# Attention heads with values held in the array: 64x64 quadrants and row sums on VectorE

## The chip, the cores and the metric

The kernel runs on one core of one Trainium2 chip. Its time is the device time of one execution, in microseconds (us). TensorE is PE in the profile and its weight loads PEld; VectorE is DVE, ScalarE ACT, GpSimd POOL, and SyncE (SP) issues DMAs.

## The reference

One block: layer norm, attention against a given key and value cache, a gated feed-forward branch, and their product added to the input. All tensors are bfloat16.

```python
B, Sq, D = 1, 2048, 640
H, Sk, Dh = 32, 2048, 192          # F = 1536
xn = layernorm(x)
q = (xn @ wq) -> (H, Sq, Dh)
scores = einsum("hqd,hkd->hqk", q, k_cache) * Dh ** -0.5
p = softmax(scores)
o = einsum("hqk,hkd->hqd", p, v_cache)
s = o -> (Sq, H * Dh) @ wo
g = silu((silu(xn @ w1) * (xn @ w3)) @ w2)
out = x + s * g
```

## The kernel before

The work runs head by head. Of a head, the 2048 queries are cut into four query blocks (`qb`) of 512, and the 2048 keys into eight steps (`p`) of 256. Even and odd keys form two halves, `t` = 0 and 1, so a step has 128 keys in each half.

**A step.** `advance` emits it. `scores` (L484) computes keys by queries, `st2`: 128 keys on the partitions, two halves of 512 queries in two PSUM banks. The 192 channels are cut into three parts of 64; each part is one pair of matmuls, the two on the two row halves of the array (`ROWS`, partitions 0 to 63 and 64 to 127), one for each key half `t`. `weights` (L490) lets ScalarE take the exponential of the 128x1024 scores into the bf16 tile `pT2`. `values` (L530) multiplies the probabilities with the values: the probabilities are the stationary operand, 64 keys by 128 queries, and 193 columns stream through them, the 192 channels of `vt` and a column of ones (`set_ones`) that yields the row sums. It takes 16 matmuls a step, in pairs on the two row halves, and accumulates over all steps of a block into two tiles of two PSUM banks, `ob0` and `ob1`.

**Order.** TensorE, VectorE and ScalarE keep the program's order for what is wrapped in `pin`; other instructions, most GpSimd copies and DMA issues of later heads among them, are placed by the framework. The values of a step are cut into parts kept in the list `parts`; they are emitted some steps behind the scores, so that the exponential has time. PSUM has two `st2` tiles, which scores and projections share in turn.

**End of a block.** `evict` copies the one row half's sums out of PSUM on VectorE (L500), adds the other's (L501), takes the reciprocal of the row sums (L506) and writes the product into the staging tile `ostage` (L507), twice for a block. A store to DRAM (`o_scr`) follows for each pair of heads and block (L511).

**Beside it, in each block.** At step 1 `project_chunk` (L361) projects 512 queries of the next head with 20 matmuls into an `st2` tile; two casts bring them to SBUF (`qA` L363, `qF` L364, VectorE), and three GpSimd copies (L367 twice, L371) make `qS` and `qD`. At step 2 follow two maxima of the new queries (L375). Key maxima of the next head are six reductions (L386) in blocks 0 and 1. In odd heads the gate of a part of the feed-forward branch is computed (L460, L464, L466). At the start of a head the keys and values of the head two further are loaded (`load_head`: L116 by a transposing DMA, L119), its projection weights are loaded from GpSimd (L105), and two GpSimd copies (L136, L139) build `KM` from the keys. The bound that is subtracted in the exponential comes from the maxima, at step 2 of block 3.

After the last head the rest of the feed-forward branch and the output projection run, up to the end.

Of the kernel before, what the change touches and what calls it, by code (L numbers as in the profile page):

```python
# [16 lines left out]
P = 128  # L17
# [13 lines left out]
def _kernel_impl(ctx, tc, A_x, A_k_cache, A_v_cache, A_wq, A_wo, B_w1, B_w3, B_w2, out):  # L31
# [117 lines left out]

    def load_head(h):  # L150
        loads[h] = {**load_weights(h), **load_keys(h)}
        copy_keys(loads[h], lambda x: x)
# [3 lines left out]
    with ExitStack() as actx:  # L156
        qp = actx.enter_context(tc.tile_pool(name="qp", bufs=2))
        pp = actx.enter_context(tc.tile_pool(name="pp", bufs=4))
# [150 lines left out]
        def start_head(h):  # L309
            L = loads.pop(h)  # L310
            heads[h] = dict(
                h=h, L=L,
# [27 lines left out]
        def project_chunk(h, qb, cast=nc.vector.tensor_copy, mid=()):  # L340
# [6 lines left out]
            if h == 0 and qb > 0:  # L347
                by_halves(halves, lambda t, c: wq[:, t, c, :], qs, nc.scalar.copy if qb == 1 else nc.vector.tensor_copy, steps((parts.pop(0),), *mid))
# [8 lines left out]
            else:  # L357
                for s in range(2 * DC):
                    for t in range(2):
                        xs = xnT if s % 2 == t else xnS  # L360
                        pin(nc.tensor.matmul(halves[t], lhsT=wq[ROWS[t], s, :], rhs=xs[ROWS[t], s // 2, qs],  # L361
                                             start=(s == 0), stop=(s == 2 * DC - 1)))
            pin(cast(out=qA[:, qs], in_=halves[0]))  # L363
            pin(cast(out=qF[:, qs], in_=halves[1]))  # L364
# [107 lines left out]
        def scores(hd, qb, p, fill=(0, 0, 0), st2=None):  # L472
# [8 lines left out]
            for s, step in enumerate(steps):  # L481
                keep_busy(fill[s])
                for t, (k, q) in enumerate(step):
                    pin(nc.tensor.matmul(st2[:, t * 512:(t + 1) * 512], lhsT=k, rhs=q[ROWS[t], qs],  # L484
                                         start=(s == 0), stop=(s == 2)))
            return st2

        def weights(st2, nb):
            pT2 = pp.tile([P, 1024], BF16, tag="pT2", name="pT2")
            pin(nc.scalar.activation(out=pT2[:], in_=st2[:], func=ACT.Exp, scale=SCALE, bias=nb[:]))  # L490
            return pT2

        def evict(hd, qb, b, ob):
            h, hg = hd["h"], hd["h"] % HG
            if b == 0 and hg == 0:
                acc[qb] = stp.tile([P, 4, HG * DH], BF16, tag=f"ostage{qb}", name="ostage")
            ostage = acc[qb]
# [5 lines left out]
            def rest():  # L503
# [3 lines left out]
                pin(nc.vector.tensor_tensor(out=ostage[:, b * 2:b * 2 + 2, hg * DH:(hg + 1) * DH], in0=osum[:, :, 0:DH],  # L507
                                            in1=rl.unsqueeze(2).to_broadcast([P, 2, DH]), op=ALU.mult))
                if b == 1 and hg == HG - 1:
                    g0 = h - hg  # L510
                    acc["store"] = nc.sync.dma_start(  # L511
                        out=o_scr[qb].rearrange("(t p) c -> p t c", p=P)[:, :, g0 * DH:(g0 + HG) * DH], in_=ostage[:, :, :])
# [6 lines left out]
        def values(hd, qb, p, pT2, by_bank=False):  # L519
# [17 lines left out]
            if p == NPAIR - 1 or by_bank:  # L537
                return [lambda b=b: part((0, 1), (b,)) for b in range(2)]
            return [lambda t=t: part((t,), (0, 1)) for t in range(2)]
# [5 lines left out]
        def advance(hd, qb, p, extra=None):  # L545
            pT2 = weights(scores(hd, qb, p), hd["nb"][qb])
            parts.extend(values(hd, qb, p, pT2))
            while len(parts) > (4 if extra else 3):
                parts.pop(0)()
            if extra:  # L550
                extra()
            while late:
                late.pop(0)()

# [47 lines left out]
        def lead():  # L602
            hd, nb = heads[0], heads[0]["nb"][0]
            vals = [values(hd, 0, p, weights(st2, nb), p < 2) for p, st2 in enumerate(early)]
# [4 lines left out]
            vals.append(values(hd, 0, 3, weights(scores(hd, 0, 3), nb)))  # L609
# [3 lines left out]
            vals.append(values(hd, 0, 4, weights(st2, nb)))  # L613
# [9 lines left out]
            parts.extend(vals[4])  # L623
# [4 lines left out]
        def next_part():  # L628
            parts.pop(0)()
# [51 lines left out]
        hTp = fstack.enter_context(tc.tile_pool(name="hTp", bufs=2, side="right"))  # L681
# [8 lines left out]
        def get_hT(qb):  # L690
            if qb not in hTs:
                hTs[qb] = hTp.tile([P, FC - 1, 512], BF16, tag="hT", name="hT")
# [29 lines left out]
        def hidden_last(qb):  # L722
# [424 lines left out]
```

## Time and profile before

| what | value |
|---|---|
| median of 3 runs | 1936.98 us (1936.93 to 1937.15) |
| profiled execution: span from first to last instruction | 1935.5 us |
| granted TensorE clock | 1.000 |
| PE busy | 1927.5 us, 26720 matmuls |
| ACT busy | 1213.5 us |
| DVE busy | 1091.5 us |
| POOL busy | 457.9 us |
| DMA moved | 148.31 MB, mean 77 GB/s |

The profiled execution's own time is the 1935.5 us of its span; no other time of it is listed, and the median of the runs lies 1.5 us above it. Matmuls are pipelined, so a group's mean (377 ns for 512 columns) is longer than the spacing of its matmuls; the chain of work that ended last gives the spacing. In a row of groups stand the line, the engine, the operation, output and input names, shapes and count, then busy us and mean ns of one, then the idle time before them and what ended it.

### The profile page before, as it was taken

What the parts mean: (1) busy time and instruction counts of PE and PEld (TensorE: products, weight loads), DVE (VectorE), ACT (ScalarE), POOL (GpSimd) and SP (SyncE); (2) the same over time, 40 slices, a digit from 0 to 9 for tenths busy, and PEclk for the clock granted to TensorE, in tenths of its full rate; (3) what the DMA queues carried; (4) which work ended last, traced back from release to release, by engine and by line L of the source; (5) the groups of instructions that cost most, each with busy time, mean ns of one, the idle gap of its engine ahead of it and who ended that gap; (6) DMA issues with size and microseconds to landing.
All of it is one profiled execution on the core that took longest, in us unless ns stands there. A gap on an engine that the chain in (4) does not pass through costs nothing.

```text
span 1935.5 us, 59521 instructions
## 1 busy us (share of the span) xinstructions
PE 1927.5 (100%) x26720; PEld 1266.1 (65%) x26743; DVE 1091.5 (56%) x2240; ACT 1213.5 (63%) x1173; POOL 457.9 (24%) x757
## 2 busy tenths in 40 slices
PE   9999999999999999999999999999999999999999
PEld 5666666666666666666666677666666666454446
DVE  8665656565656565666655666656665655521111
ACT  7777777777767677777777777777777777210000
POOL 3432222222222222233222222222222220000000
PEclk9999999999999999999999999999999999999999
DMA  7621313121212222242223222213131102946763
GB/s 172 133 71 41 80 41 79 42 71 38 59 41 65 52 55 62 57 95 68 63 50 71 50 71 49 71 41 79 42 79 38 43 10 90 262 93 144 166 151 77
DMA packets 340355, 148.31 MB, mean 77 GB/s; under 512 B 291632, under 2 KB 333584, under 8 KB 340096
## 3 DMA queue, kind: packets, MB, share of 16 engines
q1 hardware_dynamic: 327152, 114.84, 25.7%
q0 software_dynamic: 8256, 24.58, 4.8%
q10 hardware_dynamic: 4688, 5.05, 0.8%
q8 instruction: 210, 3.44, 0.8%
q14 instruction: 49, 0.40, 0.1%
HBM read 54.26 MB, written 31.98 MB: 45 GB/s over the span
## 4 chain that ended last, share of the span: by engine, by line
PE 99%; ACT 0%; issue 0%; DVE 0%; POOL 0%
PE obank L530 35%; PE st L484 34%; PE ps L361 14%; PE ps_s L891 8%; PE ps_s L847 3%; PE ps_f L911 2%; PE ps_gu L704 1%; PE ps_f L927 1%; PE ps L729 0%; PE ps L330 0%; PE fill L207 0%; PE pst L272 0%; PE ps_gu L330 0%; ACT xnT L273 0%; POOL qS L367 0%
## 5 line engine op out<-in xcount | busy, mean ns | idle before, releaser
L490 ACT ACTIVATE pT<-st,nb 128x1024 bf16<-128x1024 f32 x1016 | 1130.8, 1113 | 435.1 <-PE st L484 434.7
L530 PEld LDWEIGHTS <-pT 64*128 64x128 bf16 x16384 | 713.8, 94 | 242.0 <-ACT pT L490 1.5
L530 PE MATMUL obank<-vt,pT 64*128 64x193 bf16 x16384 | 852.3, 243 | 0.2 <-ACT pT L490 0.2
L500 DVE COPY osum<-obank 128x386 f32<-128x386 f32 x256 | 142.4, 556 | 551.4 <-PE obank L530 551.4
L484 PE MATMUL st<-qS,KM 64*128 64x512 bf16 x1023 | 385.2, 377 | 0.5 <-POOL qS L367 0.5
L484 PE MATMUL st<-qD,KT 64*128 64x512 bf16 x1023 | 385.2, 377 | 0.0
L484 PE MATMUL st<-qS,KT 64*128 64x512 bf16 x1023 | 385.1, 376 | 0.1
L484 PE MATMUL st<-qA,KT 64*128 64x512 bf16 x1023 | 385.2, 377 | 0.0
L484 PE MATMUL st<-qA,KM 64*128 64x512 bf16 x1023 | 385.2, 376 | 0.0
L484 PE MATMUL st<-qF,KT 64*128 64x512 bf16 x1023 | 385.1, 376 | 0.0
L367 POOL COPY qS<-qA 64x512 bf16<-64x512 bf16 x256 | 189.4, 740 | 513.8 <-DVE qA L363 482.3
L484 PEld LDWEIGHTS <-KT 64*128 64x128 bf16 x4096 | 202.2, 94 | 135.8 <-issue 0.6
L361 PE MATMUL ps<-xnT,wq 64*128 64x512 bf16 x1240 | 288.1, 376 | 0.0
L361 PE MATMUL ps<-xnS,wq 64*128 64x512 bf16 x1240 | 287.0, 377 | 0.0
L361 PEld LDWEIGHTS <-wq 64*128 64x128 bf16 x2480 | 120.6, 94 | 116.2
L507 DVE TENSOR_TENSOR ostage<-osum,rl_all 128x384 bf16<-128x384 f32 x256 | 153.4, 599 | 8.8
L891 PE MATMUL ps_s<-oT,wo_sb 128*128 128x512 bf16 x705 | 154.9, 379 | 0.8
L501 DVE TENSOR_TENSOR osum<-osum,obank 128x386 f32<-128x386 f32 x256 | 142.6, 557 | 8.9
L891 PEld LDWEIGHTS <-wo_sb 128*128 128x128 bf16 x720 | 70.4, 98 | 85.0 <-issue 0.2
L386 DVE TENSOR_REDUCE st<-KT 128x1 f32<-128x512 bf16 (+1 forms) x189 | 122.0, 685 | 1.2
L484 PEld LDWEIGHTS <-KM 64*128 64x128 bf16 x2048 | 101.0, 94 | 16.5 <-issue 0.5
L105 POOL DMA_DIRECT2D wq<-in_A_wq_dram x62 | 45.7, 737 | 272.8 <-PE ps L361 260.4
(136 smaller groups left out, 1174.6 us busy)
## 6 DMA issues: line engine op xcount, KB each, us to landing
o_scr<-ostage SPq DMA_DIRECT2D x64, 384.0 KB, 2.8
vt<-in_A_v_cache_dram SPq DMA_DIRECT2D x62, 384.0 KB, 4.9
wo_sb<-in_A_wo_dram POOLq DMA_DIRECT2D x1, 7680.0 KB, 32.6
wq<-in_A_wq_dram POOLq DMA_DIRECT2D x31, 160.0 KB, 3.3
hT_scr<-hblk SPq DMA_DIRECT2D x16, 256.0 KB, 3.0
xnS<-xnT POOLq DMA_DIRECT2D x8, 320.0 KB, 7.0
wq<-in_B_w_dram POOLq DMA_DIRECT2D x31, 80.0 KB, 2.6
wq<-in_A_wq_dram POOLq DMA_DIRECT2D x31, 80.0 KB, 2.9
```

The lines of the kernel that those rows point to most:

```text
L105: keep(nc.gpsimd.dma_start(out=wq[ROWS[t], :, c0:c1], in_=w.rearrange("(s p) d -> p s d", p=DT)))
L361: pin(nc.tensor.matmul(halves[t], lhsT=wq[ROWS[t], s, :], rhs=xs[ROWS[t], s // 2, qs], start=(s == 0), stop=(s == 2 * DC - 1)))
L367: keep(nc.gpsimd.tensor_copy(out=qS[ROWS[t], qs], in_=qA[ROWS[1 - t], qs]))
L386: pin(nc.vector.tensor_reduce(out=heads[h]["st"][:, j, k:k + 1], in_=heads[h]["L"]["KT"][:, j, c0:c1], axis=AX.X, op=ALU.max, apply_absolu ...
L484: pin(nc.tensor.matmul(st2[:, t * 512:(t + 1) * 512], lhsT=k, rhs=q[ROWS[t], qs], start=(s == 0), stop=(s == 2)))
L490: pin(nc.scalar.activation(out=pT2[:], in_=st2[:], func=ACT.Exp, scale=SCALE, bias=nb[:]))
L500: pin(nc.vector.tensor_copy(out=osum[:], in_=ov[:, 0, :, 0:DH + 1]))
L501: pin(nc.vector.tensor_tensor(out=osum[:], in0=osum[:], in1=ov[:, 1, :, 0:DH + 1], op=ALU.add))
L507: pin(nc.vector.tensor_tensor(out=ostage[:, b * 2:b * 2 + 2, hg * DH:(hg + 1) * DH], in0=osum[:, :, 0:DH], in1=rl.unsqueeze(2).to_broadcas ...
L530: pin(nc.tensor.matmul(acc["o"][b][:, r, (j % 2) * 256:(j % 2) * 256 + DH + 1], lhsT=pT2[ROWS[r], t * 512 + j * P:t * 512 + (j + 1) * P], ...
L847: pin(nc.tensor.matmul(ps, lhsT=oT[:, k, :], rhs=wo_sb[:, k, c0:c1], start=(k == 0), stop=(k == OC - 1)))
L891: pin(nc.tensor.matmul(ps_of[d], lhsT=wo_sb[:, k, d * P:(d + 1) * P], rhs=part(k // KQ)[:, k % KQ, :], start=(k == 0), stop=(k == OC - 1)))
```

## The change

In the heads with `1 < h < H - 1` (2 to 30, 29 of the 32):

- **Values.** The values become the stationary operand, 64 keys by 64 channels, and the probabilities stream, 512 queries at a time. Each matmul works on one 64x64 quadrant of the array: row half by key rows, column half by 64 output channels (or, for the last 64 channels, by key half `t`). A step has three groups of four matmuls. The output is channels by queries, so it must be turned; channels 128 to 191 come as two partial sums on the two partition halves. The ones column isn't used.
- **Quadrants everywhere.** Scores and projections of these heads use 64x64 quadrants as well, twice as many matmuls of the same 512 columns. At a head's first steps (scores of steps 0 and 1 of block 0, and its projection) the form of the head before is kept, as that head's values are still being emitted.
- **Eviction.** ScalarE copies one bank (`oa`), VectorE copies another (`ol`) and makes two sums with the remaining banks into the bf16 tile `ot`; a transposing DMA turns it into `ox`.
- **Row sums.** The probabilities of two steps share one tile; VectorE adds the two (`pairs`), joins the pair sums of a block (`join`, three in a block), adds the two halves (`ends`), a transposing DMA turns the 512 columns into `eT`, and VectorE reduces it and takes the reciprocal (`scale`, at the earliest six steps after `ends`). GpSimd adds the partial sums of the low channels and multiplies into `ostage`. These are chores, taken from a list by `QUOTA` per step.
- **Smaller edits.** The cast into `qF` goes to ScalarE in these heads; the probability pool has three tiles of two steps in place of four of one; parts carry the block that they belong to; the store counts the heads that wrote; the pool of `hT` is opened only in head 31, block 2, where the new tiles' room is given back.

```diff
+    def in_quads(h):
+        return 1 < h < H - 1
...
-        pp = actx.enter_context(tc.tile_pool(name="pp", bufs=4))
+        pp = actx.enter_context(tc.tile_pool(name="pp", bufs=3))
...
+        def by_steps(halves, w, qs, quads):
+            for s in range(2 * DC):
+                for c in ROWS if quads else (slice(0, P),):
+                    for t in range(2):
+                        xs = xnT if s % 2 == t else xnS
+                        pin(nc.tensor.matmul(halves[t][c, :], lhsT=w[ROWS[t], s, c], rhs=xs[ROWS[t], s // 2, qs],
+                                             start=(s == 0), stop=(s == 2 * DC - 1)))
...
             pin(cast(out=qA[:, qs], in_=halves[0]))
-            pin(cast(out=qF[:, qs], in_=halves[1]))
+            pin((cast_low or cast)(out=qF[:, qs], in_=halves[1]))
...
-                for t, (k, q) in enumerate(step):
-                    pin(nc.tensor.matmul(st2[:, t * 512:(t + 1) * 512], lhsT=k, rhs=q[ROWS[t], qs],
-                                         start=(s == 0), stop=(s == 2)))
+                for c in ROWS if quads else (slice(0, P),):
+                    for t, (k, q) in enumerate(step):
+                        pin(nc.tensor.matmul(st2[c, t * 512:(t + 1) * 512], lhsT=k[:, c], rhs=q[ROWS[t], qs],
+                                             start=(s == 0), stop=(s == 2)))
...
+        def values_quads(hd, qb, p, pT2):
+            vt = hd["L"]["vt"]
+
+            def sums(b, ts, ch):
+                bank = acc["o"][b]
+                for c, (t, c0) in enumerate(zip(ts, ch)):
+                    for r in range(2):
+                        pin(nc.tensor.matmul(bank[ROWS[c], r, :], lhsT=vt[ROWS[r], t, p, c0:c0 + DT],
+                                             rhs=pT2[ROWS[r], t * 512:(t + 1) * 512],
...
+        def evict_high(hd, qb, bank):
+            acc["oa"] = aq["one"].tile([P, 512], F32, tag="oa", name="oa")
+            pin(nc.scalar.copy(out=acc["oa"][:], in_=bank[:, 0, :]))
+
+        def evict_low(hd, qb, banks):
...
+            pin(nc.vector.tensor_copy(out=ol[:], in_=banks[1][:, 0, :]))
+            pin(nc.vector.tensor_tensor(out=ot[:, 0, :], in0=oa[:], in1=banks[0][:, 1, :], op=ALU.add))
+            pin(nc.vector.tensor_tensor(out=ot[:, 1, :], in0=ol[:], in1=banks[1][:, 1, :], op=ALU.add))
+            nc.sync.dma_start_transpose(out=ox[:].rearrange("p a j c -> p (a j) c"), in_=ot[:].rearrange("p a q -> p (a q)"))
...
+        def row_sums(hd, qb, p, w):
+            sm = hd["sums"]
+
+            def pairs():
+                t = aq["tree"].tile([P, 1024], BF16, tag="tree", name="tree")
+                add(t[:], w[:, 0, :], w[:, 1, :])
+                sm.append(t)
+
+            def join():
+                b = sm.pop()
+                add(sm[-1][:], sm[-1][:], b[:])
+
+            def ends():
+                t = sm.pop()
+                e = aq["two"].tile([P, 512], BF16, tag="e", name="e")
+                add(e[:], t[:, 0:512], t[:, 512:1024])
+                eT = aq["two"].tile([P, 4, P], BF16, tag="eT", name="eT")
+                nc.sync.dma_start_transpose(out=eT[:], in_=e[:])
+                later(6, scale, eT)
+
+            def scale(eT):
...
+                pin(nc.vector.tensor_reduce(out=rs[:], in_=eT[:], axis=AX.X, op=ALU.add))
+                rl = rl_all[:, h * NQT + qb * 4:h * NQT + qb * 4 + 4]
+                pin(nc.vector.reciprocal(out=rl, in_=rs[:]))
...
+                nc.gpsimd.tensor_tensor(out=low[:], in0=ox[:, 1, :, 0:DT], in1=ox[:, 1, :, DT:P], op=ALU.add)
+                for src, c0, c1 in ((ox[:, 0, :, :], 0, P), (low[:], P, DH)):
+                    nc.gpsimd.tensor_tensor(out=ostage[:, :, hg * DH + c0:hg * DH + c1], in0=src,
+                                            in1=rl.unsqueeze(2).to_broadcast([P, 4, c1 - c0]), op=ALU.mult)
+                staged(h, qb)
+
+            later(1, pairs)
+            if p % 4 == 3:
+                later(1, join)
+            if p == NPAIR - 1:
+                later(1, join)
+                later(1, ends)
...
+        QUOTA = (2, 0, 1, 2, 1, 1, 1, 1)
```

169 lines of the change are left out of this document (126 added, 43 removed).

## The prediction

> **What bounds the kernel now.** I read the share of each engine first, then TensorE's own waits, then the chain of work that ended last, in the stretch from 300 to 1600 us, because the start and the end are other work. The columns of the first line are busy time, share of the span and instruction count.
>
> ```profile
> span 1935.5 us, 59521 instructions
> PE 1927.5 (100%) x26720; PEld 1266.1 (65%) x26743; DVE 1091.5 (56%) x2240; ACT 1213.5 (63%) x1173; POOL 457.9 (24%) x757
> ...
> PE st L484 <- POOL qS L367: 0.5, 1, 0.5
> ...
> by line: PE obank L530 42.0%; PE st L484 40.9%; PE ps L361 16.9%; PE ps L729 0.2%
> ...
> 316.17 2.16 PE ps L361 x20
> 366.86 2.16 PE ps L361 x20
> ```
>
> TensorE is never idle: all its waits in the whole run come to under 3 us, of which the largest in the attention is the 0.5 us shown. So a head lasts as long as its matmuls: 366.86 - 316.17 = 50.69 us from one projection to the same one a head later. The shares are of the 1300 us from 300 to 1600, and the steps in them follow from the counts:
>
> ```profile
> L484 PE MATMUL st<-qS,KM 64*128 64x512 bf16 x820 | 308.8, 377 | 0.0
> L530 PE MATMUL obank<-vt,pT 64*128 64x193 bf16 x13120 | 682.1, 243 | 0.0
> ...
> L530 PEld LDWEIGHTS <-pT 64*128 64x128 bf16 x16384 | 713.8, 94 | 242.0 <-ACT pT L490 1.5
> ```
>
> 820 steps of 256 keys by 512 queries. Scores: 0.409 x 1300 / 820 = 0.648 us, in three pairs of matmuls, 0.2161 us a pair. Values: 0.420 x 1300 / 820 = 0.666 us, in eight pairs (13120 / 820 = 16 matmuls), 0.0832 us a pair. The two pairs differ by 319 columns and 0.1329 us: 0.417 ns a column and 2.8 ns for each pair whatever its width.
>
> **TensorE after.** Per step the values become three groups of four matmuls of 512 columns instead of eight pairs of 193: 1536 columns against 1544 and three fixed shares against eight, that is 8 x 0.417 + 5 x 2.8 = 17.4 ns less. I take a group of four quadrants at a pair's 0.2161 us, the nearest row, since no matmul of the trace has 64 columns of weights. Scores and projections, now cut into quadrants too, then keep their time. In heads 2 to 30 there are 29 x 32 = 928 steps: 928 x 17.4 ns = 16.2 us gained, a head of 50.69 - 0.56 = 50.13 us, a query block of 12.53 us. The two switches between forms (into head 2 and head 31) I put at nothing: each is one break in a filled queue, bounded by the 0.2 us pair.
>
> Whether the four quadrants get their weights in time is a cost the trace doesn't show. A load takes 94 ns now. One behind the other within a row half, two fit under a group (188 of 216 ns); all four in one file would take 376 ns. The Trainium skill (TensorEngine Tiling (Array Packing), Restrictions) says that column tiling switches fast weight load off, and the page TensorE: Matmul & The Clock Gate, LDWEIGHTS, prices a load at its columns over 1.2 per ns: four loads of 64 columns would be an estimated 213 ns, hidden by 3 ns even in one file. No run here shows it.
>
> **VectorE, block by block.** Its rows (mean ns of one before the last bar) and the spacing of neighbours on the timeline:
>
> ```profile
> L363 DVE CAST qA<-ps 128x512 bf16<-128x512 f32 x120 | 83.0, 692 | 15.9 <-PE ps L361 0.2
> L386 DVE TENSOR_REDUCE st<-KT 128x1 f32<-128x512 bf16 x186 | 118.5, 676 | 1.1
> L464 DVE SCALAR_TENSOR_TENSOR pa<-pt,qF 64x512 bf16<-64x512 bf16 x64 | 46.2, 721 | 0.5
> L712 DVE TENSOR_TENSOR hT<-a,u 128x512 bf16<-128x512 bf16 x12 | 5.1, 424 | 0.4
> ...
> L500 DVE COPY osum<-obank x256: 550/555/561, 29.5 to 1651.1; 128x386 f32<-128x386 f32 x128
> L501 DVE TENSOR_TENSOR osum<-osum,obank x256: 556/557/558, 30.1 to 1651.7; 128x386 f32<-128x386 f32 x128
> L506 DVE RECIPROCAL rl_all<-osum x256: 153/165/169, 30.7 to 1652.5; 128x2 f32<-128x2 f32 x128
> L507 DVE TENSOR_TENSOR ostage<-osum,rl_all x256: 557/558/1426, 30.9 to 1652.7; 128x384 bf16<-128x384 f32 x128
> ...
> 926.69 0.69 DVE L363 CAST qA<-ps 128x512 bf16<-128x512 f32 x1
> 927.30 0.68 DVE L364 CAST qF<-ps 128x512 bf16<-128x512 f32 x1
> ...
> 928.64 0.67 DVE L375 TENSOR_REDUCE st<-qA 128x1 f32<-128x512 bf16 x1
> 929.33 0.68 DVE L375 TENSOR_REDUCE st<-qF 64x1 f32<-64x512 bf16 x1
> ...
> 700.00:1300.00 600.00, 600.00 (x9288) 414.33 (x9284) 370.32 (x756) 433.62 (x403) 168.46 (x277) 1.00 0.25 62
> ```
>
> An operation followed by an independent one takes 0.08 us less than its duration (0.61 for a cast of 0.69); the two maxima take 0.69 each. From 386 to 512 fp32 elements the price rises from 557 to 692 ns, 1.07 ns an element above 144 ns. The bf16 sum of 512 at 424 ns runs at half that slope, so a 1024-element bf16 sum is 144 + 1024 x 0.54 = 0.69 us, spaced 0.61.
>
> Removed per block: two each of copy, sum, reciprocal and product (0.59 + 0.59 + 0.20 + 0.48, twice: 3.72 us) and one of two casts (0.61, moved to ScalarE). Added: four sums over a pair of steps and three joins (7 x 0.61 = 4.27), the sum of the halves (0.34), the reduction of the turned sums (0.71 with its dependent reciprocal behind it, 0.20), three evictions of 512 columns (1.83). With the cast that stays (0.61) and the maxima (1.38) a block is 9.34 us. Key maxima add four of 0.60 in block 0 and two in block 1; the bound of the next head adds about 0.6 in block 3; odd heads add 1.05 a block (0.71 + 0.34, gate products). By the same count a head before takes 4 x 6.31 + 3.6 + 0.6 + 2.1 = 31.5 us, where the window gives 370.32 / 600 x 50.69 = 31.3, so the count is good to 1%. After, blocks 0 to 3 of an odd head need 12.79, 11.59, 10.39 and 10.99 us, of an even head 1.05 less, against TensorE's 12.53. Taken alone it fits, but for 0.26 us in block 0 of odd heads.
>
> **What it collides with.** L501 reads one operand from PSUM and never varies; L507 reads two from SBUF and goes up to 1426 ns. Here is one such case, both engines:
>
> ```profile
> 788.68 1.43 DVE L507 TENSOR_TENSOR ostage<-osum,rl_all 128x384 bf16<-128x384 f32 x1
> ...
> 788.66 1.03 POOL L139 COPY KM<-KT 64x1024 bf16<-64x1024 bf16 x1
> ...
> L367 POOL COPY qS<-qA 64x512 bf16<-64x512 bf16 x256 | 189.4, 740 | 513.8 <-DVE qA L363 482.3
> L371 POOL COPY qD<-qF 64x512 bf16<-64x512 bf16 x127 | 79.1, 623 | 7.4
> ```
>
> The sum waited for GpSimd's copy (to 789.69) and ended 0.42 us behind it: a sum of two SBUF tensors stands still while GpSimd works, for what is left of GpSimd's instruction less about 0.14 us. On the timeline 43 of the 256 L507 are held like this, each with a copy under way at its start. Before, two such sums stand in a block; after, eight (pairs, joins, halves). GpSimd has three copies of about 0.61 us in a block; the change gives it a sum of 256 elements and products of 512 and 256, which the trace has no row for. Lower end: a copy's price, 0.61 and twice 0.40 (from 0.61 for 512 to 1.03 for 1024 elements, 0.82 ns an element). Upper end: the two sources read in turn, 1.03 and twice 0.61. If each of the six GpSimd instructions held one sum in full, a block would lose 3 x 0.47 + 0.99 = 2.40 to 3 x 0.47 + 1.83 = 3.24 us. At the old rate, 43 / 256 of eight sums, with GpSimd busy half as long again, two of six hit. As a GpSimd copy held by one sum starts when that ends, just ahead of the next sum of a run, I take half of the middle, 1.4 us a block; the ends are 0.8 (a third of 2.40) and 2.0 (six tenths of 3.24).
>
> The Trainium skill (GPSIMD Engine Reference, Elementwise side-by-side cycle accounting) gives 2.6 cycles an element for a sum of two tensors, an estimated 1.26 us for the 512-element product and 0.70 for the others. Half of that loss is 1.8 us a block, and the time would be about 1982 us. No run here shows it yet.
>
> At 1.4, odd blocks need 14.19, 12.99, 11.79, 12.39: over 12.53 by 1.66 and 0.46. Even blocks: 13.14, the rest below: over by 0.61. Mean 1.37 us a head. What VectorE saves in light blocks is not kept, because TensorE can run ahead of it only 1.2 us: after the last value sums of a block come a projection (2.16) and one score step (0.65) before the old bank is written again, and copy and first sum of the eviction need 0.27 + 0.61 + 0.69 behind TensorE. Inside a block that margin is used up by the order: eviction, cast, chore and two maxima stand within two steps. So 29 x 1.37 = 39.7 us are lost.
>
> **The rest.** ScalarE is at 433.62 / 600, 9.2 us a block, and gets two copies of 0.59 (the row below): 10.3 of 12.53, off the path. The DMA turns are queued on SP behind key and value loads:
>
> ```profile
> L364 ACT CAST qF<-ps 128x512 bf16<-128x512 f32 x7 | 4.1, 592 | 0.0
> ...
> KT<-in_A_k_cache_dram SPq DMA_TRANSPOSE x34, 5.6
> rows<-resT SPq DMA_TRANSPOSE x15, 2.5
> ```
>
> A turn of 512 columns lands in 2.5 us (the same shape as the turned row sums), the six times larger KT in 5.6. VectorE asks for the sums six steps later, 6 x 1.30 = 7.8 us, so they are hidden; each microsecond beyond would stop VectorE in every block. The smaller pool of probabilities (three pairs) asks a pair sum to be done within four steps; a backlog of 1 us doesn't reach that.
>
> Sum against the profiled execution: 1935.5 - 16.2 + 39.7 = 1959.0; the median of the runs stands 1.5 us above that span, so **1960.5 us**.
>
> **Rivals.** First, faster: VectorE fits. If few sums meet GpSimd (under 0.5 us a block, with the margin of 1.2 us taking the single overfull block 0 of odd heads), TensorE never waits and the whole 16.2 us stay: 1920.8 us. For it: the bare count fits everywhere but by 0.3 us. Against: GpSimd's work grows by 1.4 to 2.3 us a block while exposed sums go from two to eight. It decides at a stall of 16.2 / 29 = 0.56 us a head. Second, no change: 0.8 us a block gives 13.59 in one odd block, 0.53 a head, 1936.2 us; the same comes if a group of four costs its fixed 2.8 ns twice (232 groups a head, 0.65 us) and nothing stalls, 1939.6. Third, quadrants slower than pairs: weight loads in one file, 376 ns a group, make a head 232 x 0.376 = 87 us and the kernel about 2990 us; anything above 218.5 ns a group loses. Against it: the loads of the values already overlap, at 94 ns each with two per 83 ns. Late turns belong here too: 2 us over the 7.8 in every block are 29 x 4 x 2 = 232 us.
>
> **Numbers.** A measurement here tells about 0.2% from no change. VectorE behind, slower: 0.49, its own range 1936 to 1993 (0.8 to 2.0 us a block: at 2.0 odd heads lose 3.8 and even ones 1.2, mean 2.5, or 56 us net). Fits, faster: 0.33. No change: 0.05. Quadrants or turns slower: 0.13. The range runs from 1919 to 2000, leaving out the third rival and the tail of the first case.
>
> **What would show it.** Right: TensorE's groups at 0.216 us; waits of TensorE on VectorE's eviction sums and the cast of qA, more in odd heads; bf16 sums with a median of 0.69 us and a tail beyond 1 us beside GpSimd; VectorE near 95% busy. Wrong: TensorE without waits and heads of 50.1 us; or groups above 0.22 us with no waits; or VectorE waiting for DMA at the reduction.

## The result, and the profile after

The kernel after takes 2302.68 us (median of 4 runs, 2299.11 to 2307.44), the kernel before 1937.07 us: 1.1889 times as long, 95% interval 1.1871 to 1.1907. The prediction was 1960.5 us, with a range to 2000. The sign was right; 342 us were not foreseen. The busy times on the page, with their shares of the span of 2305.8 us:

```profile
PE 2009.6 (87%) x30896; PEld 1229.1 (53%) x30919; DVE 1637.5 (71%) x2704; ACT 1316.1 (57%) x1405; POOL 910.1 (39%) x1105
```

TensorE, never idle before, is now idle for 13% of the span, and no other engine is near full. So the time goes into waits. TensorE's own waits (us in total, times, longest):

```profile
PE ps L348 <- ACT pT L500: 247.2, 29, 9.3
PE st L492 <- ACT qF L371: 36.8, 71, 0.6
PE obank L570 <- DVE ot L602: 3.8, 12, 0.4
```

One wait in each of the 29 heads, 8.5 us long, makes most of it: the projection in block 0 needs the PSUM tile that the first exponential of the head has not yet read. The waits that the prediction named are the two small ones: 3.8 us on the eviction sums, and 36.8 us on ScalarE's cast of `qF`, which itself mostly waits for VectorE's cast of `qA`. What ScalarE waits for, and what GpSimd waits for:

```profile
ACT pT L500 <- POOL nb L447: 267.3, 29, 9.9
```

```profile
POOL ostage L644 <- issue: 192.3, 27, 7.8
POOL nb L447 <- issue: 191.7, 29, 7.7
```

The exponential waits for the bound `nb`, which GpSimd sums over the partitions (`partition_all_reduce`, L447). And GpSimd stands still twice in a head for a reason that the profile shows as "issue": no semaphore holds it. The chain that ended last, and GpSimd's timeline (start, us, engine, line, operation), at one head's start:

```profile
873.66 0.16 DVE ns L444
...
886.57 0.41 POOL nb L447
...
887.01 1.12 ACT pT L500
...
888.18 4.48 PE ps L348 x40
```

```profile
877.34 1.36 POOL L644 TENSOR_TENSOR ostage<-ox,rl_all 128x512 bf16<-128x512 bf16 x1
878.66 2.00 POOL L644 TENSOR_TENSOR ostage<-low,rl_all 128x256 bf16<-128x256 f32 x1
886.57 0.40 POOL L447 PARTITION_ALL_REDUCE nb<-ns  x1 [5.91 <-issue]
...
894.80 0.61 POOL L378 COPY qD<-qF 64x512 bf16<-64x512 bf16 x1
902.61 1.03 POOL L644 TENSOR_TENSOR ostage<-ox,rl_all 128x512 bf16<-128x512 bf16 x1 [7.20 <-issue]
```

VectorE has the bound's input ready at 873.82. GpSimd, which keeps its order, first makes copies and products up to 880.66, then stands for 5.91 us, and delivers at 886.98, 13 us later. The gap returns, 7.20 us long, ahead of the next product. The projection behind the wait takes 4.48 us, not 2.16, because TensorE's clock has fallen meanwhile, in this table of stretches (us, then busy time of PE, PEld, DVE, ACT, POOL, the granted clock, and two columns on DMA):

```profile
840.00:875.00 35.00, 33.35 (x604) 20.87 (x600) 33.05 (x55) 26.60 (x29) 17.87 (x20) 1.00 0.25 45
888.20:892.60 4.40, 4.40 (x44) 2.47 (x47) 1.28 (x2) 1.42 (x2) 2.65 (x5) 0.50 1.74 217
```

VectorE's sums and the reduction of the turned sums, as groups, then the DMA turn (count, median us from issue to landing):

```profile
L611 DVE TENSOR_TENSOR tree<-pT 128x1024 bf16<-128x1024 bf16 x464 | 383.1, 850 | 72.1 <-ACT pT L500 69.8
L611 DVE TENSOR_TENSOR tree<-tree 128x1024 bf16<-128x1024 bf16 x348 | 304.1, 874 | 8.2
...
L637 DVE TENSOR_REDUCE rs<-eT 128x4 f32<-128x512 bf16 x116 | 78.4, 676 | 20.4 <-DMA eT<-e 20.4
```

```profile
eT<-e SPq DMA_TRANSPOSE x116, 3.0
```

The sums take 850 and 874 ns where the count had 690. VectorE waits for the turned sums here and there (20.4 us in all), though the turn itself lands in 3.0 us.

### The profile page after: what moved, and what is told of

It is laid out like the page before. It is cut to its first block, busy times and chain, and to the rows that moved or that the text cites. A ratio compares the mean times of both kernels' runs of the same rounds, so it can differ in the third digit from the quotient of the medians.

```text
span 2305.8 us, 69273 instructions
## 1 busy us (share of the span) xinstructions
PE 2009.6 (87%) x30896; PEld 1229.1 (53%) x30919; DVE 1637.5 (71%) x2704; ACT 1316.1 (57%) x1405; POOL 910.1 (39%) x1105
## 4 chain that ended last, share of the span: by engine, by line
PE 48%; DVE 30%; issue 9%; DMA 6%; ACT 6%; POOL 1%; SPq 0%; POOLq 0%
PE st L492 15%; DVE tree L611 13%; PE obank L570 10%; PE ps L348 7%; PE ps_s L1056 7%; ACT pT L500 5%; DMA KT<-in_A_k_cache_dram 3%; PE obank L550 3%; DVE ol L601 3%; DMA eT<-e 2%; PE ps_s L1012 2%; DVE st L382 2%; DVE qA L370 2%; DVE ot L603 2%; DVE ot L602 2%
## 5 line engine op out<-in xcount | busy, mean ns | idle before, releaser
L570 PE MATMUL obank<-pT,vt 64*64 64x512 bf16 x11136 | 791.5, 377 | 4.1 <-DVE ot L602 3.8
L348 PE MATMUL ps<-xnT,wq 64*64 64x512 bf16 (+1 forms) x2390 | 346.8, 431 | 240.0 <-ACT pT L500 240.0
L570 PEld LDWEIGHTS <-vt 64*64 64x64 bf16 x11136 | 393.1, 107 | 241.0 <-DVE ot L603 23.5
L492 PE MATMUL st<-qS,KM 64*64 64x512 bf16 (+1 forms) x1951 | 419.0, 381 | 37.6 <-ACT qF L371 36.8
L611 DVE TENSOR_TENSOR tree<-pT 128x1024 bf16<-128x1024 bf16 x464 | 383.1, 850 | 72.1 <-ACT pT L500 69.8
L492 PE MATMUL st<-qA,KT 64*64 64x512 bf16 (+1 forms) x1951 | 417.7, 378 | 0.0
L492 PE MATMUL st<-qD,KT 64*64 64x512 bf16 (+1 forms) x1951 | 416.5, 377 | 0.0
L492 PE MATMUL st<-qA,KM 64*64 64x512 bf16 (+1 forms) x1951 | 396.6, 382 | 0.0
L492 PE MATMUL st<-qS,KT 64*64 64x512 bf16 (+1 forms) x1951 | 392.9, 378 | 0.1
L492 PE MATMUL st<-qF,KT 64*64 64x512 bf16 (+1 forms) x1951 | 391.7, 377 | 0.0
L642 POOL TENSOR_TENSOR low<-ox 128x256 f32<-128x256 bf16 x116 | 105.3, 908 | 513.4 <-DMA ox<-ot 359.4
```

The source lines that it names most:

```text
L348: pin(nc.tensor.matmul(halves[t][c, :], lhsT=w[ROWS[t], s, c], rhs=xs[ROWS[t], s // 2, qs], start=(s == 0), stop=(s == 2 * DC - 1)))
L492: pin(nc.tensor.matmul(st2[c, t * 512:(t + 1) * 512], lhsT=k[:, c], rhs=q[ROWS[t], qs], start=(s == 0), stop=(s == 2)))
L570: pin(nc.tensor.matmul(bank[ROWS[c], r, :], lhsT=vt[ROWS[r], t, p, c0:c0 + DT], rhs=pT2[ROWS[r], t * 512:(t + 1) * 512], start=(p == 0 and ...
L611: pin(nc.vector.tensor_tensor(out=out, in0=a, in1=b, op=ALU.add))
L642: nc.gpsimd.tensor_tensor(out=low[:], in0=ox[:, 1, :, 0:DT], in1=ox[:, 1, :, DT:P], op=ALU.add)
```

## The experiments

Four suspicions follow from these lines: (1) GpSimd is late with the bound, because of its queue or because of the gaps; (2) VectorE is too full, by its own count or by collisions; (3) the turns are late; (4) the quadrants are slower than counted. In the runs a block is the time from one projection to the next; it was 12.67 us before.

**e1: the bound without the sum over partitions.** From the bound of head 3 on, GpSimd copies `ns` in place of summing it over the partitions (the sum is left out).

```diff
-            keep(nc.gpsimd.partition_all_reduce(nb[:], ns[:], P, bass_isa.ReduceOp.add))
+            if 0 in heads: keep(nc.gpsimd.partition_all_reduce(nb[:], ns[:], P, bass_isa.ReduceOp.add))
+            else: nc.gpsimd.tensor_copy(out=nb[:], in_=ns[:])
```

> The changed kernel, but from head 2 on the bound is not summed over the partitions: GpSimd copies each partition's own part in place of the all-reduce (this leaves out that sum). Reload theory (GpSimd exchanges its program between its tensor sums and the all-reduce, 5.9 us before the bound and 7.2 us before the next product, and TensorE, 8.5 us without work, then runs at half clock for some 4 us): both idle stretches go, the wait at each head's start goes, and the time falls by about 29 x 11 us to 1985. Queue theory (the bound stands behind GpSimd's products in its order, no exchange needed): the bound comes at most 6 us earlier, some 3 us of wait stay at each head's start, and the time stays above 2100. Theory on record (VectorE is late in the blocks and nothing else): 2303, unchanged.

Measured: 2097.27 us, ratio 1.0819 (1.0801 to 1.0838), 205 us less. TensorE's wait at the head's start falls from 247.2 to 55.1 us. The gaps are gone with the all-reduce alone, while the products stay, as the reload theory had it. But the time is 112 us above that theory's 1985 and just under the 2100 of the queue theory, and of the wait at the head's start 1.9 us a head are left: the copied bound still stands behind GpSimd's products. The chain at a late block shows a further cause:

```profile
572.02 8.89 DMA KT<-in_A_k_cache_dram
...
587.22 1.62 POOL ostage L647 x2
...
588.86 0.39 SPq L517
...
589.35 3.74 DMA eT<-e
...
593.11 0.70 DVE rs L640
```

On SP the turn of the row sums (`eT`) stands behind the store of `ostage` (L517), which waits for GpSimd's products, which here wait behind GpSimd's copies of late keys. VectorE then waits at the reduction (L640).

**e2: the scaling on VectorE.** The all-reduce stays; the sum of the low halves and the two products go to VectorE.

```diff
-                nc.gpsimd.tensor_tensor(out=low[:], ...)      # and both products into ostage
+                pin(nc.vector.tensor_tensor(out=low[:], ...)) # and both products into ostage
```

> The changed kernel with the three operations of GpSimd per block (the sum of the low channels, the two products into the staging tile) done by VectorE instead; the all-reduce stays. Reload theory: with no tensor sum on GpSimd there is nothing to exchange, the bound is early, the wait at the head's start goes. VectorE gets about 1.4 us a block more, but fewer collisions: blocks of 13 to 14.5 us, 29 heads at some 53 us: 1990 to 2010. Queue theory: the same for the wait, since the products leave GpSimd's queue too. Theory on record: more work on the engine that is late, slower than 2303.

Measured: 2035.95 us, 1.0506 (1.0489 to 1.0524). The gaps are gone here too, with the all-reduce in place: the bound waits only for VectorE.

```profile
POOL nb L447 <- DVE ns L444: 30.7, 31, 2.4
```

```profile
L611 DVE TENSOR_TENSOR tree<-pT 128x1024 bf16<-128x1024 bf16 x464 | 319.9, 718 | 20.3 <-ACT pT L500 19.6
L611 DVE TENSOR_TENSOR tree<-tree 128x1024 bf16<-128x1024 bf16 x348 | 239.6, 689 | 8.2
```

It takes both, arithmetic and all-reduce, to make the gaps. Without GpSimd's products the sums cost 718 and 689 ns. The time is above the expected 1990 to 2010. VectorE's two products take 1076 and 811 ns and its low sum 446, 2.33 us a block where 1.4 had been expected.

**e3 and e11: the kernel before with one small GpSimd instruction a head.** A sum of 128x1 elements (e3), or a copy of 128x1 (e11), in heads from 2 on:

```diff
+            if h > 1 and qb == 1:
+                tiny = stt.tile([P, 1], F32, tag="tiny", name="tiny")
+                nc.gpsimd.tensor_tensor(out=tiny[:], in0=qA[:, 512:513], in1=qA[:, 513:514], op=ALU.add)   # e3
+                nc.gpsimd.tensor_copy(out=tiny[:], in_=qA[:, 512:513])                                     # e11
```

> The kernel before with one GpSimd sum of 128x1 elements added per head (at block 1, nobody waits for it). Reload theory: two exchanges a head, each leaving GpSimd idle for 6 to 7 us; the bound, which was 3.4 us early, comes 2 to 3 us late and TensorE loses 2 to 4 us a head: 1995 to 2055. Queue theory and theory on record: an operation of 0.2 us on an engine that is 24% busy costs nothing: 1937.

> The kernel before with one GpSimd copy of 128x1 elements added in each head from 2 on, where the earlier experiment had a 128x1 sum. Theory (only the change between a two-source sum and the all-reduce costs the 6 to 7 us): within 0.2% of 1937 us, and no row of GpSimd's bound or copy with an idle time of 6 us ahead of it. Rival (any further GpSimd instruction at that place delays the bound): about 1985 us.

Measured: e3 1986.92 us, 1.0252 (1.0230 to 1.0274); e11 1936.94 us, 0.9998 (0.9989 to 1.0008). A sum that runs 0.19 us costs the tuned kernel 1.7 us a head on the mean, a little less than the 1995 to 2055 that the reload theory expected; a copy at the same place costs nothing. GpSimd's waits in e3:

```profile
POOL nb L443 <- issue: 95.1, 16, 6.0
...
POOL tiny L374 <- issue: 48.7, 7, 7.0
```

In the other heads the profile puts stretches of the same length down to a VectorE instruction that happened to end last (13 of 6.1 us before the bound, 21 of 7.1 before the small sum). So GpSimd pays about 6 us when it goes from arithmetic to the all-reduce, and about 7 us on the way back.

**e4: e1 without the seven pair and join sums.** `pairs` hands on the tile, `join` drops one, `ends` adds the two halves of the last pair's first step (so the row sums are not the reference's); 28 of VectorE's instructions a head go.

```diff
-                add(t[:], w[:, 0, :], w[:, 1, :])
-                add(sm[-1][:], sm[-1][:], b[:])
-                add(e[:], t[:, 0:512], t[:, 512:1024])
+                add(e[:], w[:, 0, 0:512], w[:, 0, 512:1024])
```

> As the kernel without the all-reduce (copy in its place), and the seven pair and join sums of a block left out as well (the row sums are taken from the last pair of steps alone). VectorE then needs about 5 us a block, TensorE 12.53. If groups of four quadrants really take 0.216 us and only VectorE and the bound stood in the way: heads of 50.1 us and 1921. If the quadrants cost more than the pairs: above 1937 with no waits of TensorE. Theory on record: the third of the loss that it named, 1921.

Measured: 1979.98 us, 1.0218 (1.0200 to 1.0237), 59 us above the expectation. Most blocks take 12.61 us, but in nearly every second head one takes longer, in most of these 14 to 19: the turn behind the store again, 4.88 us in the chain. That led to the next pair.

**e5 and e6: the store on GpSimd's queue.** e5 is e1, e6 is e4, with this:

```diff
-                acc["store"] = nc.sync.dma_start(
+                acc["store"] = (nc.gpsimd if in_quads(h) else nc.sync).dma_start(
```

> The kernel without the all-reduce (copy in its place), and the store of the staging tile issued from GpSimd's queue instead of SP's in heads 2 to 30. Queue theory (in the kernel without the all-reduce the chain of waits runs key load, GpSimd's copies of keys, its products, SP's store, the turn of the row sums behind that store, VectorE's reduction, TensorE): VectorE's waits for the turned sums (48.8 us in 24 times) go, and with them 45 to 70 us: 2030 to 2050. Rival (VectorE is simply overfull in the blocks): 2097, unchanged.

> The kernel without the all-reduce and without the seven pair and join sums, the store issued from GpSimd's queue. Queue theory: the long blocks of every second head (15 to 17.5 us) become 12.6 like the others; 29 heads of 50.85 us: 1941 to 1945. Rival (something else makes them long): 1980, unchanged.

Measured: e5 2056.67 us, 1.0621 (1.0604 to 1.0639), 40.6 less than e1 and a little less gain than expected; e6 1941.14 us, 1.0021 (1.0011 to 1.0030), 38.8 less than e4, as expected. The queue's order is thus worth about 40 us with or without the sums. e6 shows TensorE's own price, from the starts of the projections in the chain:

```profile
1027.45 2.18 PE ps L348 x40
1040.45 2.16 PE ps L348 x40
1053.06 2.16 PE ps L348 x40
1065.67 2.16 PE ps L348 x40
1078.28 2.18 PE ps L348 x40
```

Blocks of 13.00, 12.61, 12.61 and 12.61, a head of 50.83 us against 50.69 before: 29 x 0.14 = 4.1 us, just what e6 lies above the kernel before. The quadrants gain 0.06 us in a clean block.

**e7 and e9: e5 without GpSimd's products.** Sum and products are cut to one element each, one fill of `ostage` follows. In e9 the small product writes into `ostage`, so that the fill stays behind it.

```diff
-                nc.gpsimd.tensor_tensor(out=low[:], ...)      # 128x256, and both products, 128x512 and 128x256
+                nc.gpsimd.tensor_tensor(out=low[:, 0, 0:1], ...)
+                nc.gpsimd.tensor_tensor(out=low[:, 0, 1:2], ...)                      # e7
+                nc.gpsimd.tensor_tensor(out=ostage[:, 0, hg * DH:hg * DH + 1], ...)   # e9
+                nc.gpsimd.memset(ostage[:, :, hg * DH:(hg + 1) * DH], 0.5)
```

> As the kernel without the all-reduce with the store on GpSimd's queue, and GpSimd's sum and two products of a block cut to one element with one fill of the staging tile in their place (this leaves out the scaling). Collision theory (VectorE's two-source sums stand still while GpSimd works): the pair and join sums, 913 and 807 ns there, come down to 700 to 770, and some 1.2 us a block are won: 1965 to 1995. Rival (the sums are slow by themselves, the engine is full): they stay above 800 ns and the time moves by less than 15 us.

> The kernel with the bound copied and the stores on GpSimd's queue, with GpSimd's sum and products of the scaling cut to one element each and one fill of the output stage put behind the products by the order of writes (so the outputs are not scaled). It is the experiment without products once more, without its ten fills and stores in a row. Theory (the two-source sums of VectorE stand still beside GpSimd's two-source work): pair and join sums near 0.75 us instead of 0.92 and 0.82, heads of 51.0 to 52.3 us, 1937 + 29 x 0.95 = about 1965 us, 1955 to 1975. Rival (VectorE is too full by its own count of instructions, whatever GpSimd does): still about 2055 us. Rival (the stalls of 31 and 61 us were no matter of the fill's place): above 2020 us with the same two stalls.

Measured: e7 2069.75 us, 1.069 (1.0673 to 1.0708), a miss; e9 1966.33 us, 1.0165 (1.0133 to 1.0196), as expected. In e7 the fills waited for nothing but earlier stores, and around 127 and 200 us GpSimd ran rows of fills and stores ahead of the weights of the next head; two blocks took 44 and 74 us, while later heads took 51.0 to 53 us with a single exception of 55. With that mended, e9 says what the products cost. The 464 sums over pairs of steps in e5, then in e9 (ns, minimum/median/maximum):

```profile
L614 DVE TENSOR_TENSOR tree<-pT x464: 670/930/1530, 129.6 to 1711.4; 128x1024 bf16<-128x1024 bf16 x155
```

```profile
L614 DVE TENSOR_TENSOR tree<-pT x464: 670/685/1547, 129.9 to 1624.1; 128x1024 bf16<-128x1024 bf16 x155
```

From e5 to e9 90.3 us go. One part of that is the collision. The Trainium skill (SBUF — State Buffer, Who interferes with whom) says that a VectorE instruction with two SBUF inputs and a GpSimd instruction that reads SBUF exclude each other, and that the later one waits. The trace agrees: the median goes from 930 to 685 ns when GpSimd's reads are cut.

The other part is GpSimd's queue. In e5 the copied bound still stands behind the products, ScalarE waits for it and TensorE for ScalarE; e9 has neither wait:

```profile
PE ps L348 <- ACT pT L503: 54.0, 29, 2.7
```

```profile
ACT pT L503 <- POOL nb L450: 72.3, 28, 3.4
```

By the starts of the projections the last of a head's four blocks, up to the next head's projection, shrinks from 15.04 us in e5 to 12.61 in e9 (mean of 29 heads); the other three shrink by 0.11, 0.01 and 0.52 us. So most of the 90.3 us stand, in e5, in the block with the wait for the bound.

**e8: the bound on TensorE.** The kernel complete, stores as in e5; from head 3 on the bound is summed by four matmuls of one column at step 5 of block 3, and by a copy and a sum on VectorE.

```diff
+            for c in ROWS:
+                for r in range(2):
+                    pin(nc.tensor.matmul(ps[c, r * 512:r * 512 + 1], lhsT=ones_bf[ROWS[r], c], rhs=hd["ns"][ROWS[r], :], ...
...
+                    if 1 < h < H - 1 and (qb, p) == (NQB - 1, 5): send_bound(h + 1)
```

> The changed kernel with nothing left out: the bound's sum over the partitions made by four matmuls of one column each on TensorE (they take a scores tile for a moment, at step 5 of block 3), and the store issued from GpSimd's queue. If exchange and queue order are the causes, it stands within 30 us of the kernel without all-reduce and with the store moved: 2035 to 2075. If the all-reduce mattered by its queue place only: above 2150.

Measured: 2037.05 us, 1.0518 (1.0500 to 1.0535), as expected: 266 us less than the kernel after, and everything is computed. Against e5 it gains only 19.6 us: the last block falls from 15.04 to 13.75 us, but the second rises from 13.87 to 14.61. That fits a delay of VectorE which the wait for the bound had in part covered.

**e10: the scaling on ScalarE.** Complete; all-reduce on GpSimd, the low sum on VectorE, eight scaled copies on ScalarE, stores as in e5.

```diff
+                    for j in range(4):
+                        pin(nc.scalar.mul(out=ostage[:, j, hg * DH + c0:hg * DH + c1], in_=src[:, j, :], mul=rl[:, j:j + 1]))
```

> The changed kernel complete, but GpSimd does no two-source work in the heads: the sum of the low halves is VectorE's, the scaling is eight copies with a factor on ScalarE, the sum over partitions for the bound stays on GpSimd, stores on GpSimd's queue. Theory (exchange of programs, collisions, and the turn behind the store are the whole loss): no waits of about 6 us on GpSimd, pair and join sums near 0.75 us, ScalarE up by about 2 us a block (10.1 to 12.1 of 12.61), VectorE up by about 0.45 us a block; 1965 us plus at most 29 x 4 x 0.45 = 52: 1965 to 2015 us. Rival (ScalarE becomes the bound: its copies stand ahead of the exponentials): TensorE waits on pT in each block, above 2030 us. Rival (the exchange comes with the all-reduce whatever else GpSimd does): above 2080 us.

Measured: 2142.2 us, 1.1059 (1.1040 to 1.1077): the rival. No gaps, but ScalarE is over its block:

```profile
L645 ACT ACTIVATE ostage<-ox,rl_all 128x128 bf16<-128x128 bf16 x464 | 147.3, 396 | 1.5 <-DVE rl_all L639 1.5
L645 ACT ACTIVATE ostage<-low,rl_all 128x64 bf16<-128x64 f32 x464 | 122.3, 339 | 0.0
```

```profile
PE obank L570 <- ACT pT L500: 176.3, 113, 1.6
```

Four copies of 396 ns and four of 339 are 2.94 us a block in one lump, where 2 had been assumed; blocks take 14.37 us.

**e12: GpSimd scaling with one tensor.** As e10, the eight products on GpSimd, each of one tensor and a factor per partition.

```diff
+                        nc.gpsimd.tensor_scalar(out=ostage[:, j, hg * DH + c0:hg * DH + c1], in0=src[:, j, :],
+                                                scalar1=rl[:, j:j + 1], scalar2=None, op0=ALU.mult)
```

> The changed kernel complete, the sum over partitions for the bound on GpSimd, stores on GpSimd's queue, the sum of the low halves on VectorE; GpSimd scales with eight products of one tensor and one factor per partition (four of 128 columns, four of 64) in place of products of two tensors. Theory 1 (what holds VectorE's sums and what changes programs is GpSimd's two-tensor form): no idle time of 6 us ahead of the bound, pair and join sums 0.72 to 0.76 us, heads as in the run with the fill in order (50.7 to 52.8 us) plus up to 0.45 us a block for the low sum: 1965 to 2015 us. Theory 2 (any arithmetic on GpSimd, not its copies, changes programs against the all-reduce): idle times of 5.9 and 7.2 us stay, above 2050 us. Theory 3 (any GpSimd time holds VectorE alike): eight products of 0.3 us, 2.4 us a block, hold the sums as before; sums at 0.82 to 0.92 us and 2040 to 2070 us without idle times of 6 us.

Measured: 2228.29 us, 1.1497 (1.1478 to 1.1517): theory 2 on the gaps, theory 1 on the sums.

```profile
POOL ostage L645 <- issue: 199.7, 28, 7.7
POOL nb L447 <- issue: 198.2, 29, 7.8
```

```profile
L611 DVE TENSOR_TENSOR tree<-pT 128x1024 bf16<-128x1024 bf16 x464 | 326.4, 725 | 101.6 <-ACT pT L500 101.5
L611 DVE TENSOR_TENSOR tree<-tree 128x1024 bf16<-128x1024 bf16 x348 | 244.4, 702 | 8.2
```

The gaps come with this form of arithmetic as well. The sums are hardly held any more, though GpSimd's work on a block goes from 3.3 to 6.0 us.

**e13 and e14: all three causes removed.** e13 is e12 with e8's bound on TensorE; e14 moves one eviction copy to ScalarE besides.

```diff
-            pin(nc.vector.tensor_copy(out=ol[:], in_=banks[1][:, 0, :]))
+            pin(nc.scalar.copy(out=ol[:], in_=banks[1][:, 0, :]))          # e14
```

> The complete change with all three suspected causes gone: the bound summed by four one-column matmuls on TensorE (no all-reduce from head 2 on, so no change of programs), GpSimd scaling with eight products of one tensor and a factor per partition, the low sum on VectorE, stores on GpSimd's queue. Theory (the three are the whole loss): blocks of 12.61 to 13.1 us but for block 3 with the bound at 13.2 to 13.6, heads of 51.0 to 52.0 us, 1937 + 29 x 0.8 = about 1960 us, 1945 to 1980. Rival (GpSimd's time of 5 us of products a block is itself too long, or holds VectorE once the pace is up): sums above 0.80 us, 2000 to 2040 us. Rival (VectorE's own count with the low sum is the limit): sums at 0.70 to 0.72 us, but TensorE waits on eviction sums in most blocks, 1980 to 2000 us.

> As e13, with one of VectorE's three evictions of 512 columns (the copy of the low half) moved to ScalarE: VectorE 0.6 us a block less, ScalarE 10.1 to 10.7 us of 12.6. If what remains of e13's loss is VectorE's count: 10 to 25 us faster than e13, and at best 29 x (50.44 + 0.4 - 50.69) = 4 us above the kernel before: 1938 to 1950 us. If what remains stands in TensorE, GpSimd or the bound: within 5 us of e13. If ScalarE becomes late as in the run with the scaling there: above e13.

Measured: e13 2001.59 us, 1.0332 (1.0318 to 1.0346), e14 1981.70 us, 1.0236 (1.0222 to 1.0250). Both kernels compute everything. e12 and e13 differ by the bound alone: 226.7 us. e13 lies above the expected range of the theory and by 2 us above that of the rival on VectorE's count. By its time it falls to the rival on GpSimd's products (2000 to 2040), whose sign is absent: the sums take 764 and 720 ns, not above 800. e14, 19.9 us faster, says that VectorE's count was part of the rest, but its absolute time was missed by 32 us. The starts of the projections in e14's chain show why:

```profile
700.05 2.18 PE ps L348 x40
727.40 2.16 PE ps L348 x40
740.01 2.16 PE ps L348 x40
753.38 2.16 PE ps L348 x40
779.09 2.16 PE ps L348 x40
```

The block with the bound's matmuls takes 13.37 us (740.01 to 753.38), 0.76 above a clean one: 22 us over 29 heads. Blocks 0 and 1 together take 27.35 in the head that starts at 700.05 and 25.71 in the next, in place of 25.22: VectorE, with the key maxima and, in every second head, the gate. No complete version here beats the kernel before; what the quadrants can give, if nothing else waits, is 29 x 4 x 0.06 = 7 us.

## Why the prediction was wrong

The loss of 365.6 us divides along the chain of runs, each step by one edit:

| step | us | what goes |
|---|---|---|
| after to e1 | 205.4 | all-reduce of the bound: gaps, half clock, part of the wait in the queue |
| e1 to e5 | 40.6 | turn behind the store on SP |
| e5 to e9 | 90.3 | GpSimd's products: ahead of the bound in the queue, and beside VectorE's sums |
| e9 to e6 | 25.2 | seven sums a block (with GpSimd's products back) |
| e6 to before | 4.1 | the rest |

The shares hold for this order of steps, since a wait that goes lets another show: the all-reduce is worth 205.4 us here and 226.7 from e12 to e13. The kernel after has a division of its own. Its blocks, from the projection at a head's start on, take 14.68, 13.71, 13.14 and 21.85 us (mean of 29 heads). Of the 12.94 us above four clean blocks, 9.24 lie in the block that waits for the bound and 2.07 in the next, which begins with the projection at half clock; the two others have 1.63. The sign of the forecast was right, but most of the loss lies on a way that the forecast does not have.

**The step that failed: GpSimd was costed only as a neighbour of VectorE.** Its three new instructions a block were priced by their duration and by what they hold up on VectorE. What they stand ahead of on GpSimd's own queue was not followed, and there lies the bound of the next head, for which ScalarE waits from 877.76 on, 4 us after its input is ready. Nor was it asked whether new kinds of instruction change anything for GpSimd. The profile before had one line of that among GpSimd's waits, before the first all-reduce of the program, ahead of which stand only fills, copies and DMA issues:

```profile
POOL warm L579 <- issue: 6.0, 1, 6.0
```

e2, e3, e11 and e12 show that the gap is paid at every change between arithmetic and all-reduce, not between copies and all-reduce. The trace also has what stands at the start of a gap, on GpSimd's sequencer (POOLq; ns, then first and last start in us):

```profile
L447 POOLq MODIFY_POOL_CONFIG  x58: 1/1/6, 176.7 to 1956.5; - x58
L644 POOLq MODIFY_POOL_CONFIG  x54: 7/8/8, 191.3 to 1846.7; - x54
```

They come in pairs: 29 ahead of the all-reduce, 27 ahead of the first product and three ahead of the low sum (L642). In the quoted head they stand at 880.9 us, where the products have ended, and at 895.4, where the copies have. e3 and e12 have them in every head as well; the kernel before, e2 and e11 have them only in the first 20 us. The Trainium skill (GPSIMD Engine Reference, Instruction dispatch) gives about 6 us for the first call to a freshly loaded kernel. The size agrees with the 5.91 us; that it falls due again at each change, 29 times one way and 30 the other, is what the runs add. That the gap is the load of another program is an inference from this; the runs show the gaps, the instruction that opens them and what makes them come. How the 205 us divide between gap, queue and clock was not tried apart: of the 12.75 us in the quoted case 6.84 are queue and 5.91 gap.

**TensorE: right in kind, half in size.** Groups keep their pace: a step's twelve value matmuls take 0.65 us in e1's and the kernel after's chain, and the third rival's weight loads in one file did not come: a load of 64 columns lasts 107 ns in the kernel after, twice what the estimate of 213 ns for four had, and stays hidden. A clean block is 12.61 us, not 12.53 (in e6's chain one score step of a clean block takes 0.74 in place of 0.65 us), so 7 us were to be had, not 16.2. In e6 one block in four of 13.00 us takes that back. Its chain runs over VectorE's cast, maxima, bound and last sum to an exponential for which TensorE waits 0.2 us; the rest of its 0.39 us was not followed.

**VectorE's count and collisions: mis-sized, 39.7 us against an estimated 75 to 95.** The base price was good (0.69 us; 718 and 689 ns in e2), and so was the collision: in the kernel after 4 x (850 - 690) + 3 x (874 - 690) = 1.19 us a block, for 1.4 taken. GpSimd's products take 1.04 and 0.62 us and its low sum 0.70 in e6, where these sums are absent, at or above the upper end that was taken (1.03 and twice 0.61). What failed is the slack set against the collisions. The count let odd heads pass 12.53 us by 0.26 in one block and even ones fit, some 4 us in all; without products the sums still cost 25.2 us (e9 to e6), nearly all of it in one block of each head, the second. The next lines, starts of projections in e9's chain, have every second pair of blocks 0 and 1 at 27.56 us (485.62 to 513.18), the other at 25.88, for 25.22:

```profile
434.51 2.16 PE ps L348 x40
460.39 2.16 PE ps L348 x40
...
485.62 2.18 PE ps L348 x40
513.18 2.16 PE ps L348 x40
```

From e5 to e9 the means of the sums fall from 921 and 818 to 749 and 760 ns, 4 x 0.172 + 3 x 0.058 = 0.86 us a block, and the time by 90.3 / 116 = 0.78 us a block. That these are nearly equal does not show that collisions reach TensorE whole: 2.43 of the 3.07 us a head lie in the block that waits for the bound. e8, without that wait, is 70.7 us above e9, but pays for the bound on TensorE, some 22 us by e14. So the products without the bound behind them are worth an estimated 50 to 70 us, and with the 25.2 us of the sums 75 to 95; no run has the collisions alone.

**The turns: hidden by their duration, exposed by their queue.** 2.5 us were taken and 3.0 measured, under 7.8 us of cover. But SP's queue was only looked at for loads ahead of the turn, not for the store that the change makes wait for GpSimd. That is 40.6 us; the prediction had put late turns into a rival of 0.13.

**The list of signs** was met in part: groups of 0.217 us, sums with a median of 693 ns and a tail to 1.6 us, and, from its list for being wrong, VectorE's waits at the reduction (20.4 us). But VectorE is busy 71%, not 95%, and TensorE's waits on eviction sums come to 3.8 us. The wait that decides, through the exponential to the bound, was not on it.

## What to carry to other kernels

Before a kind of instruction is added to a queue, list what else runs there and who waits for it: a tiny GpSimd sum between all-reduces cost the kernel before 50 us, a copy nothing. A transfer is hidden only if nothing ahead of it in its queue waits for a later engine. A count of an engine's work that comes within a few per cent of the bounding engine's should be read as a loss: here the sums lost 25 us where 4 had been counted, even without GpSimd's products.

## What was not expected of the hardware

GpSimd stood 5.9 us ahead of the all-reduce and 7.2 us on the way back to arithmetic, and 6.0 and 7.0 us also for a sum of one column (e3). TensorE ran at a granted clock of 0.50 for some 4.4 us after a wait of some 9 us, and 2.16 us of projection became 4.48. Products of one tensor on GpSimd (627 and 885 ns for 64 and 128 columns in e12) hardly held VectorE's sums (725 and 702 ns), where products of two did (850 and 874); at the shorter heads of e13 it was 764 and 720, against 921 and 818 in e5. They were stretched themselves: those of 128 columns take 592 ns at best, 797 in the median and up to 1657. Why the two forms differ was not tried.
